# First weights in shorter lines, and constant matmuls in bfloat16: the first ten microseconds of a feed-forward kernel

## The chip, the cores and the metric

The kernel runs on one core of a Trainium2 chip. The metric is the device time of one execution in microseconds (us), lower is better. The profile also gives the *span*, from the first to the last instruction; it is about 1.8 us shorter than the device time. All times inside an execution count from the start of the span. A load *lands* when the semaphore that tells of its completion has its last update. A *line* is a stretch of contiguous bytes that a load moves; in these traces one packet carries one line.

## The reference

```python
B, S, D, F = 32, 32, 1024, 3584          # x: 1024 rows of 1024, all in bfloat16
def reference(x, w_gate, w_up, w_down):
    return (gelu(x @ w_gate) * (x @ w_up)) @ w_down      # gelu with approximate=True
```

The contraction of the first two products is cut into 8 blocks of 128 ("block k"). The 3584 hidden columns are cut into 28 chunks of 128 ("chunk m"). Chunks 0 to 3 make up the first group of weights.

## The kernel before

The tensor engine (PE) works almost without a pause from its first real matmul to the end (busy 294.3 of 297.6 us). The argument is about how it gets started. The parts that matter, with cuts marked:

```python
# A small helper records every operation; each engine then runs its own list, with waits on semaphores.
def load_w(eng, kind, gi, k0=0, k1=DK, r=()):          # one DMA: blocks k0..k1 of one group of 4 chunks
    c0, n, buf, s0 = groups[gi]
    src, dst = (wg_r, wg_b) if kind == "g" else (wu_r, wu_b)
    pr.add(eng, "dma_start", dst[buf][:, k0:k1, s0*P:(s0+n)*P], src[:, k0:k1, c0*P:(c0+n)*P], ...)
...
# constant matmuls, whose result is not used: with them PE came to full rate at about 3.7 to 6.8 us in
# this study's traces, without seven of them (the run no_const) at about 8.2 us
one = nc.const_aps.tensor(1.0, [P, 1], BF16).bitcast(mybir.dt.float8e4)[:, 0:1]
for n in [512] * 6 + [128] * 2:
    pr.add("pe", "matmul", ps[:, 3, 0:n], one.broadcast_to([P, 2, P]), one.broadcast_to([P, 2, n]),
           start=True, stop=True, perf_mode=mybir.MatmulPerfMode.DoubleRow, w=[("ps", 3)])
# blocks 0 and 1: plain loads; x is transposed on PE (8 small matmuls) and copied by VectorE
...
for k in range(2):
    load_w("sp", "g", 0, k, k + 1)
    load_w("act", "u", 0, k, k + 1)
# blocks 2..7 of x: transposing DMAs on the SP queue
for k0, k1 in ((2, 3), (3, 4), (4, 5), (5, 6), (6, 8)):
    load_x(0, k0, k1)
# weights of blocks 2 and 3: two pieces of 256 KB, in lines of 1024 bytes, on ScalarE's queue
load_w("act", "g", 0, 2, 4)
load_w("act", "u", 0, 2, 4)
pr.add("act", "activation", warm[:, 0:1], const0, ACTF.Gelu_apprx_tanh)   # ahead of it in the trace: ACT_TABLE_LOAD, 1.28 us
...
# then PE, for the first half of the rows: block by block, gate of chunks 0..3, up of chunks 0..3
```

Of the kernel before, what the change touches and what calls it, by code (L numbers as in the profile page):

```python
# [6 lines left out]
P = 128  # L7
BF16 = mybir.dt.bfloat16
# [96 lines left out]
def bass_standalone__geglu_ffn__sampling_kernel(  # L105
# [10 lines left out]
    _, F = w_gate.shape  # L116
    DK, TC, FM = D // P, N // P, F // P
# [8 lines left out]
    pr = _Program()  # L126

    with ExitStack() as es:
# [16 lines left out]
        ps = es.enter_context(nc.psum_tensor("ps", [P, 8, 512], FP32))  # L145
# [6 lines left out]
            for i in range(n):  # L152
                where[c0 + i] = (buf, s0 + i)

        def load_w(eng, kind, gi, k0=0, k1=DK, r=()):
            c0, n, buf, s0 = groups[gi]
            src, dst = (wg_r, wg_b) if kind == "g" else (wu_r, wu_b)
            pr.add(eng, "dma_start", dst[buf][:, k0:k1, s0 * P:(s0 + n) * P], src[:, k0:k1, c0 * P:(c0 + n) * P],
                w=[(kind, buf, s0 + i, k) for i in range(n) for k in range(k0, k1)],
                r=r, dma=f"w{kind}{gi}_{k0}")  # L160

        def held_matmul(eng, out, lhsT, rhs, start, stop):
            return eng.add_instruction(mybir.InstMatmult(  # L163
# [20 lines left out]
                r=[("gb", g), ("ps", bu)], w=[("h", m, h)])  # L184


        one = nc.const_aps.tensor(1.0, [P, 1], BF16).bitcast(mybir.dt.float8e4)[:, 0:1]
        pr.add("pool", "memset", ident[:, :], 0.0, w=["id0"])
        pr.add("pool", "affine_select", ident[:, :], ident[:, :], [[-1, P]], ALU.not_equal, 1.0,
               base=0, channel_multiplier=1, r=["id0"], w=["ident"])  # L190
        for n in [512] * 6 + [128] * 2:
            pr.add("pe", "matmul", ps[:, 3, 0:n], one.broadcast_to([P, 2, P]), one.broadcast_to([P, 2, n]), start=True, stop=True,
                   perf_mode=mybir.MatmulPerfMode.DoubleRow, w=[("ps", 3)])



# [3 lines left out]
        for k in range(NX):  # L200
            load_w("sp", "g", 0, k, k + 1)
            load_w("act", "u", 0, k, k + 1)
        def load_x(h, k0, k1, r=()):
            pr.add("sp", "dma_start_transpose", xT[:, k0:k1, h * 512:(h + 1) * 512],
                   xf[h * 512:(h + 1) * 512, k0 * P:k1 * P], r=r, w=[("x", k, h) for k in range(k0, k1)],
                   dma=f"x{k0}_{h}")

        for k0, k1 in ((2, 3), (3, 4), (4, 5), (5, 6), (6, 8)):
            load_x(0, k0, k1)
        load_w("act", "g", 0, 2, 4)  # L210
        load_w("act", "u", 0, 2, 4)
        pr.add("act", "activation", warm[:, 0:1], const0, ACTF.Gelu_apprx_tanh)
        for k in range(NX):
            for i, b in enumerate((6, 7) if k == 0 else (4, 5)):
                half = ps[:, b, 0:P].bitcast(BF16)
                for t in range(2):
# [3 lines left out]
                       w=[("x", k, 0) if i == 0 else ("x", k, "b")])  # L220
# [30 lines left out]
        for m in range(4, FM):  # L251
# [12 lines left out]
            if m >= 4 and m % 3 == 0 and wd_pieces:  # L264
                a, b_ = wd_pieces.pop(0)
                pr.add("sp", "dma_start", wd[:, a:b_, :], wd_r[:, a:b_, :],
                       r=[("h", m - 1, 1)], w=[("wd", i) for i in range(a, b_)], dma=f"wd{a}")
# [6 lines left out]
        for job in jobs:  # L274
            for m in range(FM):
                for i, (tc, col, n) in enumerate(job):
# [3 lines left out]
                           r=[("h", m, tc // 4), ("wd", m)], w=[("ps", b)])  # L280
            for tc, col, n in job:
# [4 lines left out]
                else:  # L286
                    pr.add("dve", "tensor_copy", osb[:, tc, col:col + n], ps[:, b, 0:n], **keys)
                pr.add("sp", "dma_start", out_r[:, tc, col:col + n], osb[:, tc, col:col + n],
                       r=[("o", ji)], dma="out")
# [35 lines left out]
```

## Time and profile before

| | before |
|---|---|
| device time, first session | 299.28, 300.06, 300.10, 300.16 us (median 300.08) |
| span of the profiled execution | 297.6 us |
| PE busy | 294.3 us, 99% |
| constant matmuls start at | 0.77 us |
| first real matmul starts at | 4.76 us |
| x block 2 lands at (transposing DMA) | 8.43 us |
| first matmul of block 2 starts at | 8.56 us |

The page of the kernel before shows busy time by engine, then busy tenths in 40 slices of the span, then the chain of work that ended last:

```profile
PE 294.3 (99%) x1388; PEld 78.2 (26%) x808; DVE 42.7 (14%) x68; ACT 37.3 (13%) x67; POOL 0.7 (0%) x6
...
PEclk9999999999999999999999999999999999999999
DMA  7999743006708409321030040000101101011011
...
PE 96%; DMA 2%; SPq 0%; issue 0%; ACT 0%
```

PE is busy all the time and is the chain. The DMA engines are busy for long together only in the first eighth. The row of the clock says full speed from the first slice, because the page counts the time before the trace's first clock record (full speed, at 4.27 us) as full. That is not so, as the timeline of PE in the first 10 us shows (start, extent in us, engine, line, operation, operands, count; in brackets what ended an idle stretch before it):

```profile
0.77 3.01 PE L98 MATMUL ps<-const-bfloat16-1.0 128*128 128x1024 fp8e4 x8 [0.77 <-PEq L310]
3.64 0.92 PE L98 MATMUL ps<-ident,xn 128*128 128x128 bf16 x8
4.76 1.02 PE L98 MATMUL ps<-xT,wg 128*128 128x512 bf16 x4 [0.20 <-DVE xT L98]
5.62 1.03 PE L98 MATMUL ps<-xT,wu 128*128 128x512 bf16 x4
6.49 1.03 PE L98 MATMUL ps<-xT,wg 128*128 128x512 bf16 x4
7.35 1.03 PE L98 MATMUL ps<-xT,wu 128*128 128x512 bf16 x4
8.56 1.02 PE L98 MATMUL ps<-xT,wg 128*128 128x512 bf16 x4 [0.19 <-DMA xT<-in_x_dram]
```

Four real matmuls start within 0.86 us, one every 0.216 us. The six long constant ones started every 0.427 us: PE ran at half its rate then, as the small transposes show too, whose spacing falls from 0.107 to 0.056 us. In this execution the rate doubled at 4.27 us; this moment is called the release of the clock below. The bracket on the last line understates the wait, because a matmul's modelled end (0.38 us after its start) lies after the earliest start of the next (0.216 us after it): the next could have started at 7.35 + 0.86 = 8.21 and started at 8.56, so 0.35 us were lost. The chain of waits of the first 20 us names the cause (start, length, what):

```profile
2.21 6.22 DMA xT<-in_x_dram
8.43 0.14 issue
8.56 11.60 PE ps L98 x53
```

### The profile page before, as it was taken

To read this page: it belongs to the slowest core of one execution; us is meant where nothing else is said; L and a number is where in the kernel's file an instruction comes from. 1 tells how busy PE (TensorE), PEld (TensorE's weight loads), DVE (VectorE), ACT (ScalarE), POOL (GpSimd) and SP (SyncE) were. 2 spreads that over 40 slices of the span, in tenths; PEclk is the share of its full clock that TensorE was granted. 3 is DMA by queue.
4 is the path that set the end of the run, shared out by engine and by line. 5 is a ranking of instruction groups with operands and counts; after the bars stand their busy time and mean duration, and the time that the engine had idled before them with its cause. 6 is when DMAs were issued, how large, how long until landed. Compare 5 with 4: busy or idle time off the path is not lost.

```text
span 297.6 us, 2575 instructions
## 1 busy us (share of the span) xinstructions
PE 294.3 (99%) x1388; PEld 78.2 (26%) x808; DVE 42.7 (14%) x68; ACT 37.3 (13%) x67; POOL 0.7 (0%) x6
## 2 busy tenths in 40 slices
PE   8999999999999999999999999999999999999997
PEld 4444322222222222222222222222222222222244
DVE  1030311111221111111111122110000000000000
ACT  1030411111111111221111111110000000000010
POOL 0000000000000000000000000000000000000000
PEclk9999999999999999999999999999999999999999
DMA  7999743006708409321030040000101101011011
GB/s 207 252 241 353 226 134 134 9 0 189 234 2 270 154 2 330 94 76 65 0 139 4 0 141 0 0 2 0 35 0 35 37 0 35 0 37 35 0 35 35
DMA packets 28842, 26.37 MB, mean 89 GB/s; under 512 B 8352, under 2 KB 25248, under 8 KB 28832
## 3 DMA queue, kind: packets, MB, share of 16 engines
q1 hardware_dynamic: 26640, 24.25, 26.3%
q10 hardware_dynamic: 2192, 1.97, 2.2%
q8 instruction: 8, 0.13, 0.2%
q14 instruction: 2, 0.02, 0.0%
HBM read 22.28 MB, written 2.10 MB: 82 GB/s over the span
## 4 chain that ended last, share of the span: by engine, by line
PE 96%; DMA 2%; SPq 0%; issue 0%; ACT 0%
PE ps L98 54%; PE ps L163 42%; DMA xT<-in_x_dram 2%; SPq L98 0%; ACT xT L98 0%
## 5 line engine op out<-in xcount | busy, mean ns | idle before, releaser
L98 PE MATMUL ps<-xT,wg 128*128 128x512 bf16 x256 | 90.2, 379 | 0.4 <-DVE xT L98 0.2
L98 PE MATMUL ps<-xT,wu 128*128 128x512 bf16 x256 | 90.2, 379 | 0.0
L98 PE MATMUL ps<-wd,hT 128*128 128x512 bf16 (+2 forms) x280 | 86.6, 358 | 0.0
L163 PE MATMUL ps<-wd,hT 128*128 128x512 bf16 x196 | 74.3, 379 | 0.0
L163 PE MATMUL ps<-xT,wg 128*128 128x512 bf16 x192 | 72.8, 379 | 0.0
L163 PE MATMUL ps<-xT,wu 128*128 128x512 bf16 x192 | 72.8, 379 | 0.0
L98 DVE TENSOR_TENSOR hT<-g,ps 128x512 bf16<-128x512 f32 x56 | 36.4, 685 | 158.5 <-PE ps L98 158.5
L98 ACT ACTIVATE g<-ps 128x512 f32<-128x512 f32 x56 | 30.8, 595 | 160.4 <-PE ps L98 160.4
L98 PEld LDWEIGHTS ps<-wd,hT 128*128 128x128 bf16 x280 | 26.0, 98 | 71.3 <-issue 65.8
L98 PEld LDWEIGHTS ps<-xT,wu 128*128 128x128 bf16 x256 | 25.0, 98 | 71.7 <-issue 64.1
L98 PEld LDWEIGHTS ps<-xT,wg 128*128 128x128 bf16 x256 | 24.9, 98 | 72.0 <-issue 64.8
L98 DVE CAST xT<-ps 128x512 bf16<-128x512 f32 (+1 forms) x8 | 5.4, 680 | 89.6 <-ACT xT L98 79.8
L98 ACT ACTIVATE xT<-ps 128x512 bf16<-128x512 f32 (+1 forms) x9 | 5.0, 558 | 94.6 <-PE ps L98 94.6
L98 PE MATMUL ps<-const-bfloat16-1.0 128*128 128x1024 fp8e4 (+1 forms) x8 | 3.0, 558 | 0.8 <-PEq L310 0.8
L98 PEld LDWEIGHTS ps<-const-bfloat16-1.0 128*128 128x256 fp8e4 x8 | 1.7, 218 | 1.9 <-issue 1.9
L98 ACT ACT_TABLE_LOAD x1 | 1.3, 1283 | 3.4 <-issue 3.4
L98 DVE COPY xT<-ps 128x256 bf16<-128x256 bf16 x4 | 0.9, 286 | 4.1 <-PE ps L98 4.1
L98 PE MATMUL ps<-ident,xn 128*128 128x128 bf16 x8 | 0.9, 278 | 0.0
L98 PEld LDWEIGHTS ps<-ident,xn 128*128 128x128 bf16 x8 | 0.6, 124 | 0.2
L98 POOL TENSOR_SCALAR_AFFINE_SELECT ident<-ident 128x128 bf16<-128x128 bf16 x1 | 0.3, 292 | 0.2 <-POOL ident L98 0.2
L98 POOL MEMSET ident<- 128x128 bf16 x1 | 0.2, 204 | 0.3 <-POOLq L310 0.3
L98 ACT ACTIVATE warm<-const-float32-0.0 128x1 f32<-128x1 f32 x1 | 0.2, 202 | 0.0
(4 smaller groups left out, 0.4 us busy)
## 6 DMA issues: line engine op xcount, KB each, us to landing
wd<-in_w_down_dram SPq DMA_DIRECT2D x7, 1024.0 KB, 5.4
wg<-in_w_gate_dram SPq DMA_DIRECT2D x6, 1024.0 KB, 7.4
wu<-in_w_up_dram SPq DMA_DIRECT2D x6, 1024.0 KB, 9.7
out_dram<-xT SPq DMA_DIRECT2D x15, 128.0 KB, 1.7
wg<-in_w_gate_dram ACTq DMA_DIRECT2D x3, 256.0 KB, 4.5
wu<-in_w_up_dram ACTq DMA_DIRECT2D x3, 256.0 KB, 4.9
wg<-in_w_gate_dram SPq DMA_DIRECT2D x2, 128.0 KB, 3.2
wu<-in_w_up_dram ACTq DMA_DIRECT2D x2, 128.0 KB, 3.5
```

The costliest lines, as they stand in the source:

```text
L98: ins = name(eng, *args, **kw) if callable(name) else getattr(eng, name)(*args, **kw)
L163: return eng.add_instruction(mybir.InstMatmult(start_tensor_calc=start, stop_tensor_calc=stop, ldweights=False, name=nc.get_next_instructi ...
```

## The change

The intent: let the first weights come in shorter lines and smaller pieces, so that they disturb the transposing loads of x less and are usable chunk by chunk; and make the constant matmuls plain bfloat16 ones.

```diff
-        def load_w(eng, kind, gi, k0=0, k1=DK, r=()):
+        def load_w(eng, kind, gi, k0=0, k1=DK, r=(), part=None):
             c0, n, buf, s0 = groups[gi]
+            if part is not None:
+                c0, n, s0 = c0 + 2 * part, 2, s0 + 2 * part
...
-        one = nc.const_aps.tensor(1.0, [P, 1], BF16).bitcast(mybir.dt.float8e4)[:, 0:1]
+        one = nc.const_aps.tensor(1.0, [P, 512], BF16)
...
-            pr.add("pe", "matmul", ps[:, 3, 0:n], one.broadcast_to([P, 2, P]), one.broadcast_to([P, 2, n]), start=True, stop=True,
-                   perf_mode=mybir.MatmulPerfMode.DoubleRow, w=[("ps", 3)])
+            pr.add("pe", "matmul", ps[:, 3, 0:n], one[:, 0:P], one[:, 0:n], start=True, stop=True, w=[("ps", 3)])
...
-        load_w("act", "g", 0, 2, 4)
-        load_w("act", "u", 0, 2, 4)
+        for kind in "gu":
+            for part in range(2):
+                load_w("act", kind, 0, 2, 4, part=part)
```

So four pieces of 128 KB in packets of 512 bytes replace two of 256 KB in packets of 1024 bytes. Nothing else is edited.

More of the change, by code (lines that the diff above doesn't have):

```diff
@@ L159, in load_w @@
                 w=[(kind, buf, s0 + i, k) for i in range(n) for k in range(k0, k1)],
-                r=r, dma=f"w{kind}{gi}_{k0}")
+                r=r, dma=f"w{kind}{gi}_{k0}_{part}")
         def held_matmul(eng, out, lhsT, rhs, start, stop):
```

## The prediction

> **What bounds the kernel now.** The tensor engine. The summary of engines has PE busy 294.3 of 297.6 us (99%); the chain that ended last is 96% PE matmul, 2% "DMA xT<-in_x_dram". 512-column matmuls start every 0.216 us, so only fill and tail can change, and the diff touches only the fill.
>
> **The fill (timeline, records of single instructions and packets).** Constant matmuls start at 0.77 us, one every 0.427 us, the last at 3.47; the matmul transposes at 3.64, when x has landed (3.60). Their spacing drops from 0.107 to 0.056 us at 4.3 us, so the array is at full rate before the first real matmul (4.76). After block 1 the next matmul could start at 8.21, but block 2 starts at 8.56, right after the transposing load of x block 2 lands (8.43). This stall of 0.35 us is the only one in the fill. The gate weights of blocks 2-3 landed at 6.72, the up weights at 8.28, before their use (8.56, 9.43).
>
> **What the change does.**
> 1. Weights of blocks 2-3: 1024 packets of 512 bytes replace 512 of 1024. Here a 1024-byte packet takes 46 ns, a 512-byte one 27: (1024 x 27 - 512 x 46)/16 = 0.25 us more work for the 16 DMA engines. But from 5.0 to 7.0 us full engines take 256-byte transpose packets (18 ns) one for one with weight packets (about 60 of each per 0.25 us). [...] With 512-byte packets a pair costs 45 instead of 64 ns, so x block 2's 512 packets should be read about 0.5 us earlier (estimate: at most 512 x 19/16 = 0.6) and land at 7.9-8.1 instead of 8.43. That removes 0.2 to 0.35 us; 0.35 is the ceiling.
> 2. The up weights land at 8.0 to 8.8; needed from 9.1. Blocks 4-5 landed 1.35 us before use and keep at least 0.8.
> 3. Two more issues on ScalarE's queue, 0.46 to 0.58 us each, move the activation table load from 3.4 to about 4.3; ScalarE next issues at 6.7. Free.
> 4. Constant matmuls in bfloat16: half the elements, same 512 output columns, still 0.427 us each; the weight loads (0.23 us) are hidden. They end near 3.5 us, and the transposes wait for x. Nothing gained. [...] I expect the same release.
>
> **Prediction.** About 0.3 us less of 300: 299.7 us, 8 in 10 between 299.0 and 300.5. The runs of before already spread over 0.9 us. Chances: faster by over 2% 0.01, within 2% 0.98, slower 0.01.
>
> **What the profile would show.** Step 1: 512-byte packets from 4.7 to 8 us at 27 ns; x block 2 landing before 8.2; block 2's first matmul near 8.25, idle before it under 0.1 us. Step 2: no new wait of PE on wg or wu. Step 3: table load near 4.3. Step 4: constant matmuls every 0.427 us, first real matmul at 4.76, spacing 0.216 from there.
>
> **What would make it wrong.** [...] If x block 2 is limited by its write side (read by 7.0, landed only at 8.43), nothing is gained. If the up weights come past 9.1 us, PE stalls there.

The sum came to about 0.3 us less, all of it from step 1 (0.2 to 0.35 us, an estimate from the packet times of the trace); steps 2 to 4 were put at nothing. Where cuts are marked, words are gone that said more than a trace of this case shows: why packets share an engine one for one, how long PE works before its clock is released, and what a later release would cost, which was named as a risk.

## The result and the profile after

The changed kernel took 299.43, 299.59, 299.90 and 300.02 us, median 299.75, against 300.08 before. The ratio was 0.9993, with a 95% interval of 0.9977 to 1.0008. Ratios in this document are the mean time of one kernel's fast runs over that of the other's fast runs of the same rounds, so not quite the ratio of the medians quoted. Every run was fast unless the text says otherwise. The median fell by 0.33 us, about the 0.3 that was forecast, but the interval includes no change at all.

The profile does not tell the forecast's story. The page of the kernel after, its engine row and its chain that ended last:

```profile
PE 294.5 (99%) x1388; PEld 77.6 (26%) x808; DVE 42.7 (14%) x68; ACT 37.3 (13%) x67; POOL 0.7 (0%) x6
...
PE 96%; DMA 2%; ACTq 1%; issue 0%; ACT 0%
PE ps L98 54%; PE ps L165 42%; DMA wu<-in_w_up_dram 2%; ACTq L98 1%; ACT xT L98 0%
```

The DMA in the chain is no longer x but the up weights. The timeline of PE after:

```profile
0.77 2.93 PE L98 MATMUL ps<-const-bfloat16-1.0 128*128 128x512 bf16 x8 [0.77 <-PEq L312]
3.50 1.06 PE L98 MATMUL ps<-ident,xn 128*128 128x128 bf16 x8
4.61 1.02 PE L98 MATMUL ps<-xT,wg 128*128 128x512 bf16 x4
5.47 1.03 PE L98 MATMUL ps<-xT,wu 128*128 128x512 bf16 x4
6.66 1.04 PE L98 MATMUL ps<-xT,wg 128*128 128x512 bf16 x4 [0.17 <-DMA wg<-in_w_gate_dram]
7.54 1.03 PE L98 MATMUL ps<-xT,wu 128*128 128x512 bf16 x4
8.40 1.03 PE L98 MATMUL ps<-xT,wg 128*128 128x512 bf16 x4
9.95 1.06 PE L98 MATMUL ps<-xT,wu 128*128 128x512 bf16 x4 [0.53 <-DMA wu<-in_w_up_dram]
```

The first real matmul starts 0.16 us earlier. Then PE waits 0.33 us for gate weights of block 1 (6.66 against 5.47 + 0.86) and 0.69 us for up weights of block 2 (9.95 against 9.26). The wait for x block 2 is gone, two others have come, and this span is 0.5 us *longer* than before. The chain of waits of the first 20 us agrees; it runs through the third of the four new pieces:

```profile
3.51 6.39 DMA wu<-in_w_up_dram
9.90 0.05 issue
9.95 10.12 PE ps L98 x46
```

Where the weights were held up can be seen in the view of windows, the row of 5 to 6 us, first before, then after (the last three columns are the clock, the time that packets were open in the DMA engines as a share, which overlapping packets can bring over 1, and GB/s):

```profile
5.00:6.00 1.00, 1.00 (x6) 0.46 (x5) 0.01 (x1) 0.00 (x0) 0.00 (x0) 1.00 1.27 294
```

```profile
5.00:6.00 1.00, 1.00 (x6) 0.49 (x5) 0.00 (x0) 1.00 (x1) 0.00 (x0) 1.00 0.57 46
```

In the changed kernel's execution the DMA engines moved 46 GB/s in this microsecond, not 294. The packet records (in the packed trace; no view prints single packets) show why: one 1024-byte packet of the gate weights of block 1 was open from 3.93 to 5.48 us (46 ns is usual), and 16 packets begun between 4.7 and 5.7 us, transposing ones and weight packets alike, all ended together between 6.26 and 6.34. In the profile of before a shorter such pause lies at 7.6 to 8.15 us, just ahead of the late x block 2.

So the question was: is either pause a property of its kernel?

### The profile page after: what moved, and what is told of

It is laid out like the page before. It is cut to its first block, busy times and chain, and to the rows that moved or that the text cites. A ratio compares the mean times of both kernels' runs of the same rounds, so it can differ in the third digit from the quotient of the medians.

```text
span 298.1 us, 2577 instructions
## 1 busy us (share of the span) xinstructions
PE 294.5 (99%) x1388; PEld 77.6 (26%) x808; DVE 42.7 (14%) x68; ACT 37.3 (13%) x67; POOL 0.7 (0%) x6
## 4 chain that ended last, share of the span: by engine, by line
PE 96%; DMA 2%; ACTq 1%; issue 0%; ACT 0%
PE ps L98 54%; PE ps L165 42%; DMA wu<-in_w_up_dram 2%; ACTq L98 1%; ACT xT L98 0%
## 5 line engine op out<-in xcount | busy, mean ns | idle before, releaser
L98 PE MATMUL ps<-const-bfloat16-1.0 128*128 128x512 bf16 (+1 forms) x8 | 2.9, 545 | 0.8 <-PEq L312 0.8
L98 PEld LDWEIGHTS ps<-const-bfloat16-1.0 128*128 128x128 bf16 x8 | 1.0, 137 | 2.4 <-issue 2.4
```

The lines of the kernel that those rows point to most:

```text
L98: ins = name(eng, *args, **kw) if callable(name) else getattr(eng, name)(*args, **kw)
```

## Theories

- **A** (the prediction): short packets let x block 2 land earlier and take away a stall of 0.35 us. Worth 0.2 to 0.35 us.
- **B**: the pauses in the DMA engines come and go from execution to execution, and the lines change nothing that can be seen.
- **C**: all of the difference between executions is made before the up matmuls of block 2. Then span = 288.13 us + start of those matmuls, and that start = first real matmul + 4.32 us of matmuls + loss to the late clock + waits for DMA.
- **D**: short packets slow the weights themselves. **E**: sharing the engines packet by packet is what makes weights and x late.

The 288.13 of theory C comes from the first two profiles: 297.6 - 9.43 and 298.1 - 9.95 both give about 288.15, and the unrounded spans 288.13 to 288.16. The 4.32 is 20 matmuls of 0.216 us.

The three later sessions ran on three different chips (2, 1 and 3). Each ratio compares runs of one session; each trace is one execution on one of these chips.

## The experiments

### The change again, its two halves, and pieces cut another way

The diff of after_again is none: it is the changed kernel.

> The changed kernel once more, for a tighter interval and a second trace. Theory A (small lines let x block 2 land earlier and remove the 0.35 us stall): 0.2 to 0.35 us faster than before in the mean; x block 2 lands before 8.2 us again; the stall on the up weights of block 2 seen in the first trace (0.69 us) is small or absent. Theory B (a DMA straggler in the first 10 us, differing from run to run, decides; the change has no effect of its own): within 0.2 us of before, and the stalls of this trace sit at other places or have other lengths than in the first trace of the same kernel.

Measured: 298.94 to 299.28, median 299.18, against 299.61 for before; ratio 0.9983 (0.9969 to 0.9998). The timeline of PE:

```profile
4.61 1.47 PE L98 MATMUL ps<-xT,wg 128*128 128x512 bf16 x4
5.92 1.03 PE L98 MATMUL ps<-xT,wu 128*128 128x512 bf16 x4
...
8.51 1.03 PE L98 MATMUL ps<-xT,wg 128*128 128x512 bf16 x4
9.37 1.03 PE L98 MATMUL ps<-xT,wu 128*128 128x512 bf16 x4
```

No wait for DMA at all. Instead the first four matmuls took 1.31 us to start, not 0.86: the first gaps are 0.380, 0.427 and 0.287 us, the half rate of the constant matmuls. The clock record says that full speed came at 5.55 us. 0.45 us went to the clock. This is theory B's sign: same kernel, other losses. The time alone would have looked like theory A.

lines_only keeps the fp8 constants:

```diff
 (the changed kernel, with)
+        one = nc.const_aps.tensor(1.0, [P, 1], BF16).bitcast(mybir.dt.float8e4)[:, 0:1]
+            ... one.broadcast_to([P, 2, P]), one.broadcast_to([P, 2, n]) ... perf_mode=DoubleRow
```

> 512-byte lines in four pieces, constants left in fp8. Theory A: keeps the whole gain, 0.2 to 0.35 us. Theory B: within 0.2 us of before; total of PE idle stretches in the first 20 us between 0.2 and 1.2 us. If the constants gave the gain, nothing is left here.

Measured: five runs of 299.21 to 299.81, ratio 0.9996 (0.9981 to 1.0011), and the profiled one of 636.57 us, slow. The line of its span and its largest groups (count, busy us, mean ns):

```profile
span 634.8 us, 2551 instructions
...
L98 PE MATMUL ps<-xT,wg 128*128 128x512 bf16 x250 | 161.5, 680 | 1.4 <-issue 1.4
L98 PE MATMUL ps<-xT,wu 128*128 128x512 bf16 x250 | 160.6, 677 | 0.8 <-issue 0.8
```

A 512-column matmul takes 0.68 us instead of 0.38, to the very end; they start 0.443 and 0.558 us apart, a pattern seen in no other trace. This spacing is there from the second constant matmul on (1.12 us), before the first weight or x packet (1.83 us), and up to there this kernel runs the same instructions as the one before. So the transfers that the edit changes are not its cause. The mean granted clock of this profile (`--cores`) is 1.000 all the same, as in the fast traces; the spacing of matmuls is the safer reading. The run is left out of all comparisons and taken up again below.

const_only is the other half: the kernel before with only the two hunks about `one`.

> Constants in bfloat16, lines of 1024 bytes as before. Theories A and B both: within 0.15 us of before; the constant matmuls end about 0.07 us earlier (second one starts at 1.15 instead of 1.23), first real matmul at 4.60 to 4.80; clock released at 4.2 to 4.6 us. If bfloat16 counted as less activity: release later than 5 us and 0.3 us or more slower.

Measured: median 299.34, ratio 0.9993 (0.9977 to 1.0009). First real matmul at 4.61, clock released at 5.40 (4.2 to 4.6 had been expected), loss 0.37 us, no wait for DMA; x block 2 landed at 7.85. The release lies in the range of the fp8 kernels (4.2 to about 6.8), so nothing points to a later release with bfloat16 constants.

by_block cuts four pieces by block, so that each keeps 1024-byte lines:

```diff
-        load_w("act", "g", 0, 2, 4)
-        load_w("act", "u", 0, 2, 4)
+        for kind in "gu":
+            for k in (2, 3):
+                load_w("act", kind, 0, k, k + 1)
```

> Four pieces too, but cut by block with 1024-byte lines: tells packet size from number of pieces. Theory A (packet size): x block 2 lands at about 8.4 as before, no gain. If smaller pieces (earlier completion of the first half) gave the gain: 0.2 us or more faster. Theory B: within 0.2 us of before.

Measured: ratio 1.0001 (0.9986 to 1.0016). x block 2 landed at 7.42 us, a full microsecond before the 8.43 of the first profile, *with 1024-byte lines*. The one reading on which theory A rested is thus not what long lines must give. This trace has the largest loss to the clock of all with constant matmuls in full number, 0.97 us:

```profile
4.76 1.87 PE L98 MATMUL ps<-xT,wg 128*128 128x512 bf16 x4
6.42 1.20 PE L98 MATMUL ps<-xT,wu 128*128 128x512 bf16 x4
7.46 1.03 PE L98 MATMUL ps<-xT,wg 128*128 128x512 bf16 x4
```

Four matmuls took 1.66 us to start, the next four 1.04; at full rate it is 0.86.

### The kernel before again, and the packet size alone

> The kernel before, once more. Theory C (span = 288.13 us + start of the first up matmul of block 2; that start = 4.76 us + 4.32 us of matmuls at full rate + what is lost until the clock is released + what PE waits for DMA): span minus 288.13 equals that start within 0.05 us; its parts differ from the first trace, where they were 0.00 (clock) and 0.35 (DMA); spans of the runs between 297.2 and 298.7.

Measured: median 299.56 against 299.42 for the same kernel in its other 11 runs, ratio 1.0010 (0.9997 to 1.0023). A kernel compared with itself thus shows how far such a ratio strays. Its timeline:

```profile
4.71 1.56 PE L98 MATMUL ps<-xT,wg 128*128 128x512 bf16 x4
6.10 1.03 PE L98 MATMUL ps<-xT,wu 128*128 128x512 bf16 x4
...
8.69 1.03 PE L98 MATMUL ps<-xT,wg 128*128 128x512 bf16 x4
9.55 1.03 PE L98 MATMUL ps<-xT,wu 128*128 128x512 bf16 x4
```

The stall on x block 2 that the prediction meant to remove is not there: x landed at 7.79, and PE, 0.53 us late through the clock, came to it only at 8.69. Span minus start is 297.7 - 9.55 = 288.1, as theory C says.

block_512 and block_256 take by_block and break its destination lines, without more DMAs, into a buffer `w23` of their own:

```diff
-                load_w("act", kind, 0, k, k + 1)
+                pr.add("act", "dma_start", w23[:, int(kind == "u"), k - 2, :, 0:C * P],   # C = 2 or 1 chunks
+                       src[:, k, 0:4 * P].rearrange("p (a f) -> p a f", a=4 // C), ...)
...
+            if m < 4 and k in (2, 3):
+                lhs = w23[:, int(kind == "u"), k - 2, m // C, (m % C) * P:(m % C + 1) * P]
```

> Same four pieces, by block, as by_block, but each in 512-byte packets: packet size alone. If small packets let x block 2 land earlier (theory A): x block 2 lands before 7.3 us (7.42 in by_block). If small packets only slow the weights (theory D): the last piece of up weights lands 0.3 to 1.0 us later than in by_block (9.12), x block 2 lands at 7.4 or later. Time within 0.5 us of before either way.

> The same in 256-byte packets, double the suspected cost. Theory A: x block 2 lands earlier still. Theory D: 2048 packets of about 18 ns are 2.3 us of 16 engines instead of 1.5, up weights of block 2 land after 9.5 us, those of block 3 after 10.5; 0.3 to 1.5 us slower than before.

| | by_block | block_512 | block_256 |
|---|---|---|---|
| usual length of a packet of blocks 2-3 | 46 ns | 27 ns | 18 ns |
| longest packet of the first 11 us | 0.68 us | 1.92 us | 0.76 us |
| x block 2 lands | 7.42 | 8.71 | 7.34 |
| up weights of block 2 / block 3 land | 8.19 / 9.12 | 10.19 / 10.76 | 8.87 / 9.49 |
| ratio to before | 1.0001 | 0.9998 (0.9985 to 1.0011) | 0.9992 (0.9980 to 1.0004) |

Neither A nor D: the landings do not follow the packet size. In these three traces they go with the longest packet, but over all traces that does not hold either: before has a longest packet of 0.53 us and x block 2 at 8.43, lines_again one of 0.50 us and x at 7.13. block_512 happened to be profiled in an execution of 298.4 us; its five other spans lie between 297.2 and 297.6. block_256, with twice the suspected cost, has a trace without any loss, against what theory D asked for (after 9.5 and 10.5 us, 0.3 to 1.5 us slower).

### A candidate to beat both

by_use joins bfloat16 constants to pieces by block in the order of use:

```diff
 (const_only, and)
-        load_w("act", "g", 0, 2, 4)
-        load_w("act", "u", 0, 2, 4)
+        for k in (2, 3):
+            for kind in "gu":
+                load_w("act", kind, 0, k, k + 1)
```

> Constants in bfloat16 with pieces of 1024-byte lines by block in the order of use: a candidate to beat both. Theory C: first real matmul at 4.61 (0.157 earlier than with fp8 constants), no wait for weights of block 2, so spans from 297.06 up; mean 0.15 to 0.35 us below before. If the constants were worth nothing: equal to before.

Measured: median 299.26, but with two runs of 300.38 and 300.80; ratio 1.0009 (0.9990 to 1.0028). Its trace has the wait for x block 2 again (landed at 8.24, 0.31 us lost). Not faster.

### Keeping weights and transposes apart, and taking the constants away

apart moves the up weights of blocks 2-3 to the SP queue, ahead of the transposing loads:

```diff
 (const_only, and)
             load_w("act", "u", 0, k, k + 1)
+        load_w("sp", "u", 0, 2, 4)
...
         load_w("act", "g", 0, 2, 4)
-        load_w("act", "u", 0, 2, 4)
```

> Constants in bfloat16, 1024-byte lines; the up weights of blocks 2-3 go on the SP queue ahead of the x transposes, so transposes and these weights no longer share an engine one for one. If the interleaving is what makes x and weights late (theory E): weights of blocks 2-3 land by 7.0 us, x block 2 by 7.7, PE waits for no DMA in the fill, only the clock costs; mean 0.2 to 0.6 us below before. If the late packets are stragglers that come whatever the order (theory B): the longest packet of the first 11 us is still over 0.5 us, and the mean stays within 0.2 us of the bfloat16 kernel with 1024-byte lines (ratio 0.9993).

Measured: the up weights landed at 7.22 and the gate weights at 7.83, not by 7.0, and x block 2 at 8.20, not by 7.7. A packet of 0.96 us was there as well, and the ratio was 1.0006 (0.9987 to 1.0025): no gain. PE waited for no DMA, but only because this trace lost 0.82 us to the clock (release at 6.31 us): it came to block 2 at 8.88, and at full rate it would have been there at about 8.06 and have waited for x. Theory E's marks are all missed but the one that PE waits for no DMA, and that one says little, as PE was late anyway.

no_const takes seven of the eight constant matmuls out of const_only:

```diff
-        for n in [512] * 6 + [128] * 2:
+        for n in [128]:
```

> All constant matmuls but one short one taken away, 1024-byte lines. Theory C ([...]each us after the first real matmul at half rate costs half): first real matmul at 4.4 to 4.7, [...]waits for DMA in block 2 gone since PE is late itself; 0.6 to 1.8 us slower than before. If the constants do not govern the release: within 0.3 us of before.

The sum, 0.6 to 1.8 us slower, came from a time of the release and a loss: they were the author's estimate and no trace had shown them.

Measured: median 300.77 against 299.51, ratio 1.0041 (1.0023 to 1.0058): the one clear difference. The timeline:

```profile
3.16 1.04 PE L98 MATMUL ps<-ident,xn 128*128 128x128 bf16 x8 [2.12 <-DMA xn<-in_x_dram]
4.25 1.87 PE L98 MATMUL ps<-xT,wg 128*128 128x512 bf16 x4
5.91 1.91 PE L98 MATMUL ps<-xT,wu 128*128 128x512 bf16 x4
7.62 1.30 PE L98 MATMUL ps<-xT,wg 128*128 128x512 bf16 x4
```

Full rate came only at about 8.2 us (worked out from the one gap of 0.276 us in which the rate changed), 5.0 us after PE's steady work began at 3.16, and 1.91 us were lost to it. The first real matmul, which had nothing ahead of it but x, started at 4.25. x block 2 landed at 8.42, as late as in the first profile of before, and cost nothing, because PE came to it at 9.62. This shows what the constants are for (full rate at about 8.2 us with one short one left, at about 3.7 to 6.8 with all eight) and that a late clock hides a late DMA.

### The change and its lines once more

> The changed kernel a third time. The first two comparisons gave ratios 0.9993 and 0.9983. Theory C with constants worth 0.10 us at the first real matmul and lines worth nothing: ratio 0.9990 to 1.0000 over many runs. Theory A: 0.9985 to 0.9993.

Measured: median 299.52 against 299.51; ratio 1.0001 (0.9985 to 1.0017). The gain of after_again did not come again. The trace has a wait for up weights like the first:

```profile
8.36 1.03 PE L98 MATMUL ps<-xT,wg 128*128 128x512 bf16 x4
9.63 1.04 PE L98 MATMUL ps<-xT,wu 128*128 128x512 bf16 x4 [0.25 <-DMA wu<-in_w_up_dram]
```

9.63 against 8.36 + 0.86 = 9.22: 0.41 us.

> Only the lines, once more, because the first profile of it fell in an execution of 634.8 us with matmuls every 0.44 to 0.56 us from the first constant one to the end. If that came from the kernel it comes again in one of the runs; if it was a state of the chip, all runs are near 299.5. Theory A: x block 2 lands before 8.1 and ratio near 0.9991. Theory C: ratio within 0.0007 of 1.

Measured: six runs of 298.93 to 299.89, ratio 0.9995 (0.9979 to 1.0011); the 636 us did not come back. In all 109 executions it came once. The trace, span 297.1 us, lost nothing to clock or DMA:

```profile
3.58 0.93 PE L98 MATMUL ps<-ident,xn 128*128 128x128 bf16 x8
4.71 1.02 PE L98 MATMUL ps<-xT,wg 128*128 128x512 bf16 x4 [0.20 <-DVE xT L98]
```

### The account, trace by trace

Loss to the clock: sum of what the gaps between the first real matmuls exceed 0.216 us, where they are 0.24 to 0.43 us and no landing ends them. Loss to DMA: the same for the gaps that end with a landing.

| trace | first real matmul | clock | DMA | up matmuls of block 2 | span |
|---|---|---|---|---|---|
| before | 4.76 | 0 | 0.35 (x block 2) | 9.43 | 297.6 |
| before_again | 4.71 | 0.53 | 0 | 9.55 | 297.7 |
| lines_again | 4.71 | 0 | 0 | 9.02 | 297.1 |
| by_block | 4.76 | 0.97 | 0 | 10.05 | 298.2 |
| block_512 | 4.71 | 0 | 1.21 (gate 1, x 2, up 2) | 10.24 | 298.4 |
| block_256 | 4.71 | 0 | 0 | 9.02 | 297.1 |
| const_only | 4.61 | 0.37 | 0 | 9.30 | 297.4 |
| by_use | 4.62 | 0 | 0.31 (x block 2) | 9.24 | 297.4 |
| apart | 4.61 | 0.82 | 0 | 9.75 | 297.9 |
| after | 4.61 | 0 | 1.02 (gate 1, up 2) | 9.95 | 298.1 |
| after_again | 4.61 | 0.45 | 0 | 9.37 | 297.5 |
| after_third | 4.72 | 0.19 | 0.41 (up 2) | 9.63 | 297.8 |
| no_const | 4.25 | 1.91 | 0 | 10.48 | 298.6 |

In each row the first three columns and 4.32 add up to the fourth, and the fourth and 288.13 to the span, within 0.05 us. The first of these sums is bookkeeping, since the losses are read off the gaps between the same matmuls. The second could have failed: the rest of the span is 288.11 to 288.15 us in all 13 traces. Theory C holds in this sense; it says where the time goes, not why a clock or a landing is late.

The first column shows what the constants are worth. Where the first half of x for blocks 0 and 1 landed by 3.5 us, bfloat16 kernels start the real work at 4.61 and fp8 kernels at 4.71. Where it landed near 3.6, x has its part in it, and the values are 4.62 and 4.72 against 4.76. Of the 0.10 us, 0.07 lie between the first two constant matmuls (0.453 us apart with fp8, 0.380 with bfloat16). The rest lies where the small transposes follow on the constants: gaps of 0.111 and 0.128 us in before_again, 0.107 each in the changed kernel. The longer fp8 weight loads (0.18 to 0.23 us against 0.11 to 0.15) would explain both places, but no run changed their length alone. In time, 0.10 us is 0.03% of 300, less than any interval here resolves (const_only: 0.9977 to 1.0009). Here is the start of const_only, to set beside lines_again:

```profile
3.50 1.06 PE L98 MATMUL ps<-ident,xn 128*128 128x128 bf16 x8
4.61 1.40 PE L98 MATMUL ps<-xT,wg 128*128 128x512 bf16 x4
```

Two things in the packet records were not used above, and no experiment was made on them. The first is where the pauses begin. Call it a pause when three or more packets stay open for over 0.3 us and end together, each within 0.12 us of the one before. In none of the 13 traces does a pause begin before the first transposing packet, though 1024-byte weight packets run for over 1 us before it. In ten traces the first pause begins 0.4 to 1.0 us after that packet; in before, lines_again and by_block it begins 2.3 to 4.0 us after. In apart, where the first transposing packet came at 5.68 us, the first pause began at 6.20; in the other nine of the ten these were 4.2 to 4.5 and 4.6 to 5.4. So the transposing loads are a suspect for the pauses; no run took them away, and the cause stays open. The second is the end of x block 2: the first 512 transposing packets, as many as it has, have all ended 0.75 to 1.4 us before it lands (7.06 against 8.43 in before). The prediction had named this ("limited by its write side") as something that would make it wrong, and it was never tested.

## Why the prediction was right or wrong

**What bounds the kernel, and that only the fill can change: right.** PE is busy 99% before and after, and the rest of the span is the same within 0.04 us in all traces of normal rate.

**The total, 299.7 us and within 2%: right, for a sum that was not made as forecast.** The median was 299.75. Three comparisons of the same two kernels gave ratios of 0.9993, 0.9983 and 1.0001. That the first median fell by just the forecast amount is luck: the profiled execution of those runs lost 1.02 us to waits that were not forecast. The change is worth a few tenths of a microsecond at most and may be worth nothing; more cannot be said with these runs.

**"This stall of 0.35 us is the only one in the fill ... 0.35 is the ceiling": this step failed.** It was true of the one execution read. The step took it for a property of the kernel. In the second profile of the same kernel there is no such stall, and 0.53 us are lost to the clock instead. The 33 spans of before in the later sessions run from 297.0 to 298.7, mean 297.7, where a trace without loss has 297.1. About 0.6 us is lost in the mean, now to one cause, now to the other, and a late clock hides a late x (in no_const x block 2 landed at 8.42 us and PE came to it at 9.62).

**x block 2 at 7.9 to 8.1 instead of 8.43: not shown.** It landed at 8.16, 7.39 and 7.76 in the three traces of the changed kernel, so the test that I had set (before 8.2) was met. But with 1024-byte lines and the same queues it landed at 7.42 to 8.43, and with 512-byte lines, block_512 included, at 7.13 to 8.71. Nor do the times of the reading itself decide it: from the start of the first to that of the 512th transposing packet it took 1.49 to 3.03 us in the six traces with shorter lines and normal rate (mean 2.2) and 2.02 to 3.02 in the six with 1024-byte lines on the same queues (mean 2.4). The half microsecond that was computed may be there, hidden by the pauses. The packet times were right (27 and 46 ns in both kernels), as was the one-for-one sharing in the first trace (62 transposing and 64 weight packets begun from 5.25 to 5.5 us, for example). What the forecast left out is the pauses of 0.5 to 1.9 us, as large as the 0.5 us that I had computed or larger.

**Up weights at 8.0 to 8.8, no new wait: wrong.** The last up piece landed at 10.36, 9.42 and 9.84, and in two of three traces PE waited for up weights, 0.69 and 0.41 us. In lines_again the last one landed at 9.03. With the two pieces of 1024-byte lines it was 8.28, 9.39, 9.13 and 9.70 (before, before_again, const_only, no_const), and no trace waited for it. The means are 9.66 and 9.13. That short lines cost the up weights their slack is possible, but the ranges overlap, four pieces with 1024-byte lines landed last at 9.12 and 9.99 (by_block, by_use), and block_256 did not show it (9.49); it stays open.

**Constants in bfloat16, "nothing gained": wrong in size.** They are 0.427 us apart from the second on, as the fp8 ones are, and bring the first real matmul forward by 0.10 us when x is early (4.61 against 4.71). The step that failed is that the transposes always wait for x, and that the constants, ending near 3.5 either way, are off the path: in eight of the twelve traces with all constants x came first and the constants decided. A DoubleRow weight load took 0.230 us here against 0.147 for a bfloat16 one, 56% more, both while PE ran at half rate (before and after); no run here has these loads at full rate.

**The clock, "the same release": wrong as a time, right that bfloat16 makes no difference that can be seen.** The release was expected where the first trace has it (4.27 us). PE begins at 0.77 us in every trace; full rate came between about 3.7 us (or a little before) and 6.8 us with the full set of constants (by the clock records, or worked out from the spacing where a trace has none: by_use and by_block, the two ends). The ranges overlap: about 3.7 to 6.31 us with bfloat16 constants (by_use, apart), 4.2 to 6.8 with fp8. The clock records of before and after have full rate for 293.546 us in both before it falls to half, while PE's last matmul starts 290.94 and 291.23 us after the release. What sets the two moments was not shown. The cost of a later release, named as a risk in words now cut, is what no_const shows: 1.91 us.

**Two more issues on ScalarE's queue are free: right, though later than said.** The new issues took 0.61 to 0.73 us each, the activation table load began at 4.87 and not 4.3, and ScalarE's next issue came at 6.53 after a wait for PE.

## What to carry to other kernels

One profile shows one execution: before a stall of a few tenths of a microsecond is made the target of a change, profile the unchanged kernel again and see whether it is still there. Write the start of a kernel as a sum (first real work + full-rate work + clock + waits) and check that it adds up in each trace, because a loss to one term can hide another, as 1.91 us of a late clock hid an x block 2 that landed at 8.42 us in no_const. Where the runs of one kernel spread over more than the expected gain, a ratio such as 0.9983 with an interval just under 1 can be luck, and here it did not come again.
